# Order of the maxima's scores against the fills in four slots, and two PSUM copies, in a sliding-window attention and MLP kernel

## The chip, the cores and the metric

One Trainium2 chip, one core of it. The core has TensorE (PE; PEld are its weight loads), VectorE (DVE), ScalarE (ACT), GpSimd (POOL) and SyncE (SP), which here issues the DMAs. The metric is device time in microseconds (us) of the whole program, the median of its runs; lower is better.

## The reference

One block of a transformer: sliding-window attention over the normalized input, gated by an MLP, in float32. S is 2048 tokens, D is 512, 32 heads of 16, a window of 256, and F is 1792.

```python
xn = _layernorm(x)
# attention: 32 heads, each query sees the 256 keys up to its own
qkv = (xn @ wqkv).reshape(B, S, 3, H, Dh)          # q, k, v by heads
scores = jnp.einsum("bhqd,bhkd->bhqk", q, k) * (Dh ** -0.5)
mask = (idx[:, None] - idx[None, :] >= 0) & (idx[:, None] - idx[None, :] < W)
p = _softmax(jnp.where(mask, scores, -1e9))
s = jnp.einsum("bhqk,bhkd->bhqd", p, v).reshape(B, S, D) @ wo
# gate: a second layer norm, Dense, GELU, Dense, SiLU
h = _gelu(_layernorm(xn) @ w1 + b1)
g = _silu(h @ w2 + b2)
return x + s * g
```

## The kernel before

The program runs in two parts. The first is attention, with everything that can be done beside it; the second is the rest of the MLP, the output projection and the gate.

**Slots.** The first part is one loop over `t` from -16 to 128, and a turn of it is called a slot here. Slots 0 to 127 are eight groups of four heads (`n = t // 16`) times sixteen blocks of 128 keys (`kb = t % 16`). In the slots below 0 the input is normalized and transposed, and the first projections run. All engines get their instructions in the order in which the loop issues them (`Ordered` keeps program order), so a line's place in the loop is its place in each engine's queue.

**Scores for the exponentials.** `prob_block(n, kb, p)` makes the scores of 128 keys against up to 384 queries for two heads: two matmuls on the two halves of the PE's rows, into `stb`, one pair of PSUM banks. ACT takes the exponential into `pt`, and POOL zeroes what lies outside the window with one or two selects. There are two such blocks in a slot, `p = 1` and then `p = 0`, and both use `stb`; from slot 116 on, the block of `p = 1` uses `xy` instead.

**Maxima.** The softmax needs each query's largest score in advance, LEAD = 12 slots ahead. `max_block(n, qb)` makes scores of a block of 128 queries in four matmuls into the pair of banks `xy`. The window's far corner comes as `first_scores` into `zo`. DVE merges the corner into `xy` with a predicated copy (`COPY_PREDICATED`; in the first two blocks of a group there is no corner, and a constant is used) and reduces `xy` to the negative maximum `mt`. `own_max(t + 12)` is the call of it in slot t. The maxima's rows are split and transposed, and travel through DRAM back into the q and k buffers.

**Fills.** Between these, PE works on other products, matmul by matmul: projections of later heads' q and k, of v, and hidden rows of the MLP. They accumulate in the banks `fb[0]` and `fb[1]` (in the profile `fb`, in the program's order `fb_111` and `fb_112`). A fill is a pair of matmuls on the two halves of PE's rows, one for each bank. `fills[t, half]` holds those of a slot: half 0 stands between the two score blocks, half 1 behind the second. `by_halves` places a job's pairs in slots that are written out by hand: the q and k projection of the second group's second chunk (`job_qk(1, 1)`) has six pairs each in slot 0 (half 1), slot 1 (half 0) and slot 2 (halves 0 and 1). `tandem(t0, t1, ...)` spreads two jobs over the slots t0 to t1 and ends them in slot t1, by copying the two banks out: `fb[0]` in half 0 and `fb[1]` in half 1, both on ACT. The next pair that writes these banks waits for the copies. Spans that end in slots 19, 35 and 115 are followed by a span that starts in the next slot.

**Copies of v.** `job_v(0, 7)` ends behind the first score block, which is issued at the end of slot -1. Its two banks are copied into `vt` on ACT (the inner `finish` of `job_v`), ahead of slot 0's exponential. The first fills of slot 0 use the same banks.

**Where the maxima stand.** In a slot, PE gets the first score block, the maxima's scores, the fills of half 0, the second score block, the fills of half 1, the corner of the next maximum, and the product of the probabilities with v for the block before (`pv_step`, into `zo`). The table `MAX_BEHIND` moves the maxima's scores of a slot behind so many of its fills of half 0: 2 in slots 1, 4, 20, 36, 52, 84 and 100, and in all other slots they stand in front.

All instructions are recorded at line 43, the line of `Ordered`, so the profile's rows are told apart by their tiles. `pjr` and `hr` are the raw copies of the fills' banks (a projection, a hidden row), `sh` is the rounded high part of a projection, `oraw` the copied product with v.

Of the kernel before, what the change touches and what calls it, by code (L numbers as in the profile page):

```python
# [17 lines left out]
S, D, H, DH, WIN, F = 2048, 512, 32, 16, 256, 1792  # L18
# [5 lines left out]
NQ = H // 4  # L24
EPS = 1e-5
NEG = -3.0e38
LEAD = 12
# [23 lines left out]
def mixer_kernel(ctx, tc, x, wqk, wv, wo, w1, b1, w2, b2, out):  # L51


    nc = SimpleNamespace(**{name: Ordered(tc, name) for name in ("tensor", "vector", "scalar", "gpsimd", "sync")})
# [131 lines left out]
    fb = [psf.tile([P, 512], F32, name=f"fb{i}") for i in range(2)]  # L186
# [10 lines left out]
    vt = vp.tile([P, NKB, 16, DH + 1], F32, name="vt")  # L197
# [92 lines left out]
    fills = {}  # L290
# [95 lines left out]
    def job_v(hf, i):  # L386

        box = []

        def mm(k):  # L390
            if k == 0:
                box.append(ps_st.tile([P, 2, 256], F32, tag="b", name=f"pv_{hf}_{i}"))
            j, kt, (a, b) = k // 12, k % 12 // 3, PASSES[k % 3]
            kb = 2 * i + j
            nc.tensor.matmul(box[0][:, j], big[:, a, kt, P * kb: P * (kb + 1)], wva[:, b, kt],
                             start=(k % 12 == 0), stop=(k % 12 == 11))

        def half(bank, j, k, r, **flags):
            kt, (a, b) = k // 3, PASSES[k % 3]
            kb = 2 * i + j  # L400
            return nc.tensor.matmul(bank[:, 0:256], big[r, a, kt, P * kb: P * (kb + 1)], wva[r, b, kt], **flags)

        def finish():
            if i < 4:
                nc.scalar.copy(vt[:, 2 * i: 2 * i + 2, :, 0:DH], box[0].rearrange("p b (h d) -> p b h d", d=DH))
                return
            for j, bank in enumerate(box):
                nc.scalar.copy(vt[:, 2 * i + j, :, 0:DH], bank[:, 0:256].rearrange("p (h d) -> p h d", d=DH))
        if i > 3:
            return half, finish, box  # L410
        return [(109, mm, k) for k in range(24)], finish
# [86 lines left out]
    def tandem(t0, t1, one, two, mid=None, back=None):  # L498

        n = one[0]
        lo, hi = slice(0, 64), slice(64, P)
        mid = mid or max(1, (t0 + t1 + 1) // 2)
        most = n // 4

        def places(slots, last):

            last = min(most, n // (len(slots) + 1)) if last else 0
            cuts = [(n - last) * k // len(slots) for k in range(len(slots) + 1)]  # L510
            out = []
            for t, a, b in zip(slots, cuts, cuts[1:]):
                ahead = min(b - a, n // 3) if t < 16 * NQ - LEAD else min(b - a, max(most, (b - a + 1) // 2))
                out += [(t, 0)] * ahead + [(t, 1)] * (b - a - ahead)
            return out + [(t1, 0)] * last

        first, second = places(range(t0, mid), False), places(range(back or mid, t1), True)
        for phase, where in enumerate((first, second)):
            for i in range(n):
                flags = dict(start=(phase == 0 and i == 0), stop=(phase == 1 and i == n - 1), skip_group_check=True)  # L520
                def unit(i=i, phase=phase, flags=flags):
                    made = ((two if phase == 0 else one)[1](fb[1 - phase], i, hi, **flags),
                            (one if phase == 0 else two)[1](fb[phase], i, lo, **flags))
                    if phase == 1 and i == 0 and t0 < 16 * NQ - LEAD:
                        for r in made:
                            tc.add_manual_dep(r.ins, outs["copy"].ins.name, ORDER, reason="the banks change rows")
                fills.setdefault(where[i], []).append((unit, ()))
        fills.setdefault((t1, 0), []).append((one[2], (fb[0], t1, nc.scalar.copy)))
        if t1 >= 16 * NQ - LEAD:
            fills[t1, 0].append((two[2], (fb[1], t1, nc.vector.tensor_copy)))  # L530
            return
        ends_pair.add(t1)

        def copy(dst, src):
            outs["second"] = nc.scalar.copy(dst, src)
        fills.setdefault((t1, 1), []).append((two[2], (fb[1], t1, copy)))

    def spread(jobs, places):

# [74 lines left out]
    def prob_block(n, kb, p):  # L614
        slot = slots[n % 2]
        w = min(384, S - P * kb)
        pt = pp.tile([P, 2, 384], F32, tag="pt", name=f"pt_{n}_{kb}_{p}")
        both = xy if p and 16 * n + kb + LEAD >= 16 * NQ else stb[0]
        for a in (1, 0):
            r = slice(64 * a, 64 * a + 64)  # L620
            nc.tensor.matmul(both[:, a, 0:w], slot[r, 1, p, P * kb: P * (kb + 1)],
                             slot[r, 0, p, P * kb: P * kb + w], start=True, stop=True)
        writers[n, kb, p] = [nc.scalar.activation(pt[:, :, 0:w], both[:, :, 0:w], AF.Exp, scale=DH ** -0.5)]
        select = nc.gpsimd.affine_select(out=pt[:, :, 0:P], in_=pt[:, :, 0:P], pattern=[[0, 2], [1, P]],
                                compare_op=ALU.is_ge, fill=0.0, base=0, channel_multiplier=-1)
        if w == 384:
            select = nc.gpsimd.affine_select(out=pt[:, :, 256:384], in_=pt[:, :, 256:384],
                                             pattern=[[0, 2], [-1, P]], compare_op=ALU.is_gt, fill=0.0,
                                    base=0, channel_multiplier=1)
        writers[n, kb, p].append(select)  # L630
        pts[(n, kb, p)] = pt
# [194 lines left out]
    del fills[-11, 1][-5:]  # L826
    soon = {}
    tandem(3, 8, pair_qk(1, 2), pair_qk(1, 3))
    for n, spans in enumerate((((9, 14), (15, 19)), ((20, 24), (25, 30)), ((31, 35), (36, 41)), ((42, 47), (48, 53, 51)),
                               ((75, 79), (80, 85)), ((86, 91), (92, 97))), 2):  # L830
        for c, span in zip((0, 2), spans):
            tandem(*span[:2], pair_qk(n, c), pair_qk(n, c + 1), *span[2:])
    for i, (t0, t1) in enumerate(((54, 58), (59, 63), (64, 68), (69, 74))):
        tandem(t0, t1, pair_v(2 * i), pair_v(2 * i + 1))
# [73 lines left out]
           -10: [ln3[0][0], ln3[1][0], ln3[0][1], ln3[1][1], ln3[0][2], ln3[1][2]],  # L908
           -9: [ln3[2][0], ln3[3][0], ln3[2][1], ln3[3][1], ln3[2][2], ln3[3][2]]}

    MAX_BEHIND = {t: 2 for t in (1, 4, 20, 36, 52, 84, 100)}

    def own_max(m):
        max_block(m // 16, m % 16, m not in IN_PLACE)

    def fill_in(t, half):
        now[:] = t, half
        run(delayed.pop((t, half), ()))
        for k, (fn, args) in enumerate(fills.get((t, half), ())):
            if half == 0 and k == MAX_BEHIND.get(t):  # L920
                own_max(t + LEAD)
# [3 lines left out]
    for t in range(-16, end + 1):  # L925
# [5 lines left out]
        if 0 < t < end:  # L931
            prob_block(t // 16, t % 16, 1)
        if t >= 0 and m < end and t not in MAX_BEHIND:
            own_max(m)
# [53 lines left out]
    for f in range(6, NF, 2):  # L988
        t = gp.tile([P, 2, 512], F32, tag="ohl", name=f"hr_{f}", bufs=4)
# [451 lines left out]
```

## Time and profile before

| | us |
|---|---|
| median of 3 runs | 731.88 (731.73 to 732.29) |
| the profiled execution | 732.0 |
| its span, first to last instruction | 730.3 |

Busy time by stretch of the span, from the windows view; the granted TensorE clock is 1.00 in each:

| stretch, us | what runs | length | PE | PEld | DVE | ACT | POOL |
|---|---|---|---|---|---|---|---|
| 0 to 63.4 | slots -16 to 0 | 63.4 | 60.8 | 56.2 | 50.1 | 48.5 | 32.4 |
| 63.4 to 72.2 | slots 1 to 3 | 8.8 | 8.4 | 6.3 | 6.6 | 6.5 | 4.5 |
| 72.2 to 386.2 | slots 4 to 115 | 314.0 | 308.9 | 244.9 | 231.0 | 239.0 | 225.9 |
| 386.2 to 413.7 | slots 116 to 127 | 27.5 | 27.4 | 19.1 | 10.1 | 20.4 | 20.4 |
| 413.7 to 730.3 | the second part | 316.6 | 312.9 | 259.0 | 197.4 | 113.5 | 40.6 |

A row of the timeline gives the start in us from the span's start, the length, the engine, the operation, its tiles as out<-in with shapes, the count of merged instructions, and in brackets the idle time of that engine ahead of it with what ended it. The weight loads (PEld) show best when PE was held, since they are not modelled as matmuls' ends are. Slot 1 begins with the stb load at 63.4, slot 20 with the stb matmul at 117.0, slot 36 at 162.6, slot 115 at 383.4.

### The profile page before, as it was taken

What the parts mean: (1) busy time and instruction counts of PE and PEld (TensorE: products, weight loads), DVE (VectorE), ACT (ScalarE), POOL (GpSimd) and SP (SyncE); (2) the same over time, 40 slices, a digit from 0 to 9 for tenths busy, and PEclk for the clock granted to TensorE, in tenths of its full rate; (3) what the DMA queues carried; (4) which work ended last, traced back from release to release, by engine and by line L of the source; (5) the groups of instructions that cost most, each with busy time, mean ns of one, the idle gap of its engine ahead of it and who ended that gap; (6) DMA issues with size and microseconds to landing.
All of it is one profiled execution on the core that took longest, in us unless ns stands there. A gap on an engine that the chain in (4) does not pass through costs nothing.

```text
span 730.3 us, 19066 instructions
## 1 busy us (share of the span) xinstructions
PE 718.3 (98%) x7584; PEld 585.4 (80%) x7584; DVE 495.0 (68%) x729; ACT 427.8 (59%) x725; POOL 323.9 (44%) x683
## 2 busy tenths in 40 slices
PE   8999999999999999999999999999999999999997
PEld 7998777777778887777776788888888888888886
DVE  7886776867766777777882657446687855667823
ACT  8767777877777676878877736232343734541001
POOL 7444767767677665777876540203303000001102
PEclk9999999999999999999999999999999999999999
DMA  8324447777776733667624366347223312263801
GB/s 302 75 50 109 100 122 180 215 226 221 207 206 175 208 123 96 171 156 211 175 90 155 104 238 204 142 131 244 87 57 116 117 58 87 67 191 108 252 18 58
DMA packets 61528, 106.77 MB, mean 146 GB/s; under 512 B 12096, under 2 KB 12352, under 8 KB 61440
## 3 DMA queue, kind: packets, MB, share of 16 engines
q1 hardware_dynamic: 61440, 105.56, 49.3%
q8 instruction: 60, 0.98, 0.6%
q14 instruction: 28, 0.23, 0.1%
HBM read 54.53 MB, written 33.82 MB: 121 GB/s over the span
## 4 chain that ended last, share of the span: by engine, by line
PE 93%; ACT 3%; DVE 2%; DMA 1%; SPq 1%; issue 1%; POOL 0%; DVEq 0%; POOLq 0%
PE acc L43 21%; PE fb L43 20%; PE zo L43 14%; PE p L43 9%; PE stb L43 9%; PE s L43 6%; PE h L43 6%; PE xy L43 5%; ACT pt L43 2%; PE pv L43 2%; DVE xy L43 1%; DVE mt L43 1%; SPq L43 1%; DMA x<-in_x_dram 1%; PE tr L43 0%
## 5 line engine op out<-in xcount | busy, mean ns | idle before, releaser
L43 POOL TENSOR_SCALAR_AFFINE_SELECT pt<-pt 128x256 f32<-128x256 f32 x480 | 193.4, 428 | 96.7 <-ACT pt L43 91.1
L43 ACT ACTIVATE pt<-stb 128x768 f32<-128x768 f32 (+1 forms) x244 | 188.7, 774 | 44.0 <-PE stb L43 37.8
L43 DVE TENSOR_REDUCE mt<-xy 128x4 f32<-128x1024 f32 (+1 forms) x128 | 152.6, 1192 | 4.4
L43 DVE COPY_PREDICATED xy<-upper,zo 128x512 f32<-128x512 int32 x112 | 77.8, 695 | 73.9 <-PE xy L43 64.8
L43 POOL TENSOR_TENSOR xo<-xo,gated 128x512 f32<-128x512 f32 x15 | 20.0, 1331 | 220.4 <-DVE gated L43 219.4
L43 PE MATMUL zo<-pt,vt 128*17 128x128 f32 x2880 | 103.7, 275 | 0.0
L43 PE MATMUL fb<-xnT,wqb 64*128 64x512 f32 (+2 forms) x732 | 100.6, 382 | 0.3
L43 PE MATMUL stb<-qk 64*128 64x384 f32 (+1 forms) x488 | 94.6, 382 | 4.6 <-ACT pt L43 3.0
L43 PE MATMUL acc<-w,gh 128*128 128x512 f32 x320 | 98.5, 389 | 0.0
L43 PEld LDWEIGHTS stb<-qk 64*128 64x128 f32 x488 | 45.7, 183 | 48.1 <-ACT pt L43 39.5
L43 PEld LDWEIGHTS zo<-pt,vt 128*17 128x17 f32 x2880 | 67.5, 97 | 15.0 <-issue 5.0
L43 PEld LDWEIGHTS acc<-w,gh 128*128 128x128 f32 x320 | 60.1, 188 | 12.5
L43 PEld LDWEIGHTS fb<-xnT,wqb 64*128 64x128 f32 (+1 forms) x732 | 62.2, 185 | 7.3 <-ACT pjr L43 0.6
L43 PE MATMUL acc<-w,gl 128*128 128x512 f32 x160 | 62.2, 389 | 0.0
L43 PE MATMUL xy<-qk 64*128 64x256 f32 (+2 forms) x536 | 57.6, 288 | 0.4 <-DVE mt L43 0.2
L43 PE MATMUL p<-xnT 128*128 128x512 f32 x189 | 51.8, 389 | 0.0
L43 PEld LDWEIGHTS xy<-qk 64*128 64x128 f32 x536 | 46.8, 185 | 5.2 <-issue 2.2
L43 ACT COPY oraw<-zo 128x128 f32<-128x128 f32 x108 | 28.8, 266 | 37.5 <-PE zo L43 28.0
L43 ACT ACTIVATE gated<-acc 128x512 f32<-128x512 f32 x16 | 8.7, 596 | 61.9 <-DVE acc L43 61.9
L43 PE MATMUL s<-wos,ohl 128*128 128x512 f32 (+1 forms) x204 | 44.3, 376 | 0.0
L43 PEld LDWEIGHTS s<-wos,ohl 128*128 128x128 f32 x204 | 36.8, 188 | 7.1
L43 PEld LDWEIGHTS p<-xnT 128*128 128x128 f32 x189 | 35.5, 188 | 7.3
(206 smaller groups left out, 1193.3 us busy)
## 6 DMA issues: line engine op xcount, KB each, us to landing
qk<-sh SPq DMA_DIRECT2D x128, 128.0 KB
qk<-pjr SPq DMA_DIRECT2D x64, 128.0 KB
oT_d<-oraw SPq DMA_DIRECT2D x32, 256.0 KB
w_d<-in_w_dram SPq DMA_DIRECT2D x14, 512.0 KB
xt_d<-xnT SPq DMA_DIRECT2D x12, 512.0 KB
x<-in_x_dram SPq DMA_DIRECT2D x16, 256.0 KB
w<-w_d SPq DMA_DIRECT2D x16, 256.0 KB
or<-oT_d SPq DMA_DIRECT2D x16, 256.0 KB
```

The source lines that it names most:

```text
L43: r = issue(*args, **kwargs)
```

## The change

Three edits.

In `job_v`, the second bank of the last v job is copied by VectorE. In `tandem`, the second bank's copy is issued in half 0 when the span ends in slot 115 (spans that end later returned before this line, and LEAD is 12, so `16 * NQ - LEAD` is 116). In `MAX_BEHIND`, the maxima's scores stand behind four pairs of fills in slot 1 (two before) and in slot 2 (none before), and in front of the fills in slots 20 and 36 (behind two before). Slots 4, 52, 84 and 100 stay.

```diff
             for j, bank in enumerate(box):
-                nc.scalar.copy(vt[:, 2 * i + j, :, 0:DH], bank[:, 0:256].rearrange("p (h d) -> p h d", d=DH))
+                copy = nc.vector.tensor_copy if i == 7 and j else nc.scalar.copy
+                copy(vt[:, 2 * i + j, :, 0:DH], bank[:, 0:256].rearrange("p (h d) -> p h d", d=DH))
...
-        fills.setdefault((t1, 1), []).append((two[2], (fb[1], t1, copy)))
+        fills.setdefault((t1, int(t1 + 1 < 16 * NQ - LEAD)), []).append((two[2], (fb[1], t1, copy)))
...
-    MAX_BEHIND = {t: 2 for t in (1, 4, 20, 36, 52, 84, 100)}
+    MAX_BEHIND = {1: 4, 2: 4, 4: 2, 52: 2, 84: 2, 100: 2}
```

On DVE in slot 0, the copy stands between the reduction of the maximum of slot -1 (`mt_8`) and the predicated copy of slot 0's:

```order
 L43 COPY_PREDICATED xy<-upper,zo 128x4x128
 L43 TENSOR_REDUCE mt_8_874<-xy 128x4
+L43 COPY vt<-fb_112 128x16x16
 L43 COPY_PREDICATED xy<-upper,zo 128x4x128
 L43 TENSOR_REDUCE mt_12_1106<-xy 128x4
```

One copy is added here, and the same copy is gone from ACT, where it stood ahead of the exponential `pt_0_0` of slot 0.

On PE in slot 20, the piece between the first score block and the rest of the fills (xy are the maxima's scores, fb the fills):

```order
 L43 MATMUL stb<-qk_751 128x384 x2
-L43 MATMUL fb_112<-xnT,wqb_1900 128x512
-L43 MATMUL fb_111<-xnT,wqb_1900 128x512
-L43 MATMUL fb_112<-xnT,wqb_1900 128x512
-L43 MATMUL fb_111<-xnT,wqb_1900 128x512
 L43 MATMUL xy<-qk_94 128x128 x4
+L43 MATMUL fb_112<-xnT,wqb_1900 128x512
+L43 MATMUL fb_111<-xnT,wqb_1900 128x512
+L43 MATMUL fb_112<-xnT,wqb_1900 128x512
+L43 MATMUL fb_111<-xnT,wqb_1900 128x512
```

Two pairs of fills moved behind the four xy matmuls; slot 36 changes in the same way. In slots 1 and 2 the movement is the other way, by two pairs and by four.

On ACT in slots 115 and 116 (`hr` are the two banks' copies, `pt_3_0` the second exponential of slot 115, `pt_4_1` the first of slot 116):

```order
 L43 ACTIVATE pt_3_1_6901<-stb 128x768
 L43 COPY hr_6919<-fb_111 128x512
-L43 ACTIVATE pt_3_0_6923<-stb 128x768
-L43 COPY hr_6929<-fb_112 128x512
+L43 COPY hr_6921<-fb_112 128x512
+L43 ACTIVATE pt_3_0_6925<-stb 128x768
 L43 ACTIVATE pt_4_1_6950<-xy 128x768
```

The exponential now stands behind both copies. The other engines' orders stay as they were.

## The prediction

> **What bounds the kernel now.** I read the page's engine row first, then the waits, then the timeline of the slots that the change touches. The page's first row and its engine row, then rows of the waits view (engine, what waits, on whom: us in total, times, longest):
>
> ```profile
> span 730.3 us, 19066 instructions
> PE 718.3 (98%) x7584; PEld 585.4 (80%) x7584; DVE 495.0 (68%) x729; ACT 427.8 (59%) x725; POOL 323.9 (44%) x683
> ...
> PE stb L43 <- DMA qk<-mT_d: 0.6, 1, 0.6
> ...
> PEld stb L43 <- ACT pt L43: 39.5, 149, 0.9
> ...
> PEld xy L43 <- DVE mt L43: 1.1, 3, 0.5
> ...
> PEld fb L43 <- ACT pjr L43: 0.6, 2, 0.3
> ...
> PEld fb L43 <- ACT hr L43: 0.3, 1, 0.3
> ```
>
> PE looks busy 98% of the time, but a matmul's end is modelled, so the waits must be read at the weight loads (PEld). There the score blocks of the exponentials (stb) wait 149 times for ACT: they share one pair of banks, so block, exponential and next block alternate. The other three kinds of wait are few, and the change aims at them.
>
> How long that alternation takes is seen in slots 35 to 37, in the timeline (start, length, engine, what, idle time before it):
>
> ```profile
> 161.39 1.23 DVE L43 TENSOR_REDUCE mt<-xy 128x4 f32<-128x1024 f32 x1
> ...
> 161.77 0.82 ACT L43 ACTIVATE pt<-stb 128x768 f32<-128x768 f32 x1
> ...
> 162.64 0.44 PE L43 MATMUL stb<-qk 64*128 64x384 f32 x2 [0.18 <-ACT pt L43]
> ...
> 163.12 0.30 PEld L43 LDWEIGHTS fb<-xnT,wqb 64*128 64x128 f32 x4 [0.29 <-ACT pjr L43]
> ...
> 163.12 0.81 ACT L43 ACTIVATE pt<-stb 128x768 f32<-128x768 f32 x1
> ...
> 164.75 0.81 ACT L43 ACTIVATE pt<-stb 128x768 f32<-128x768 f32 x1 [0.31 <-PE stb L43]
> ...
> 165.62 0.18 PEld L43 LDWEIGHTS stb<-qk 64*128 64x128 f32 x2 [0.41 <-ACT pt L43]
> ```
>
> From one exponential's start to the next takes 1.35 us at least (161.77 to 163.12): 0.82 of ACT, 0.05 to release PE, 0.44 of matmuls and 0.04 back. A slot has two, so nothing goes below 2.70 us per slot. Where an exponential starts later than 1.35 us after the one before, PE or another engine was late, and only that surplus can be won. Slot 36 shows it: 164.75 - 163.12 = 1.63, a surplus of 0.28, and ACT says that it waited 0.31 for PE. PE was late because the first fill pair of the slot stood 0.29 us for ACT's copy of the bank.
>
> **Slots 0 to 2.** The rows of these slots:
>
> ```profile
> 61.76 0.65 ACT L43 COPY vt<-fb 128x256 f32<-128x256 f32 x2 [0.99 <-PE fb L43]
> ...
> 62.19 0.70 DVE L43 COPY_PREDICATED xy<-upper,zo 128x512 f32<-128x512 int32 x1 [1.20 <-PE zo L43]
> 62.41 0.81 ACT L43 ACTIVATE pt<-stb 128x768 f32<-128x768 f32 x1
> 62.46 0.77 PEld L43 LDWEIGHTS fb<-xnT,wqb 64*128 64x128 f32 x12 [0.35 <-ACT vt L43]
> ...
> 63.68 0.40 PE L43 MATMUL fb<-xnT,wqb 64*128 64x256 f32 x4
> 63.88 0.81 ACT L43 ACTIVATE pt<-stb 128x768 f32<-128x768 f32 x1 [0.66 <-PE stb L43]
> ...
> 64.20 0.30 PEld L43 LDWEIGHTS xy<-qk 64*128 64x128 f32 x4 [0.33 <-DVE mt L43]
> ...
> 65.39 0.81 ACT L43 ACTIVATE pt<-stb 128x768 f32<-128x768 f32 x1 [0.70 <-PE stb L43]
> ...
> 66.74 0.81 ACT L43 ACTIVATE pt<-stb 128x768 f32<-128x768 f32 x1
> 66.75 0.30 PEld L43 LDWEIGHTS xy<-qk 64*128 64x128 f32 x4 [0.31 <-DVE mt L43]
> ...
> 67.10 0.88 PE L43 MATMUL fb<-xnT,wqb 64*128 64x256 f32 x12
> ...
> 68.19 0.81 ACT L43 ACTIVATE pt<-stb 128x768 f32<-128x768 f32 x1 [0.65 <-PE stb L43]
> ```
>
> Here the maxima set the pace. The xy scores wait for the reduction before them in slot 1 (0.33) and slot 2 (0.31), and what is queued behind them on PE, fills and the second stb block, waits too.
>
> *Slot 0.* A VectorE copy of 256 elements from PSUM has no row. These are the nearest, from the groups by shape (count, busy, mean ns):
>
> ```profile
> L43 DVE COPY oraw<-zo 128x128 f32<-128x128 f32 x20 | 5.8, 290 | 1.9 <-PE zo L43 0.5
> ...
> L43 DVE TENSOR_TENSOR hr<-fb,scales 128x512 f32<-128x512 f32 x4 | 2.6, 686 | 16.1 <-PE fb L43 11.5 <-PE stb L43 4.6
> ```
>
> The bounds are 0.29 and 0.69; by length, 0.29 + (0.69 - 0.29) x 128/384 = 0.42, which I take. DVE is idle then and starts at 61.76, when ACT starts the first bank, so it is done at 62.18, and the predicated copy behind it moves from 62.19 by 0.02 or so (by 0.29 at the upper bound, by nothing at the lower). The fills begin at 62.22 and not at 62.46. The exponential of 62.41 keeps its place, since its block on PE comes no earlier. The next may start at 62.41 + 1.35 = 63.76, 0.12 earlier than 63.88.
>
> [...]
>
> *Slot 1.* A pair of fills costs (0.88 - 0.40)/4 = 0.12 (six pairs against two). The xy scores still wait for the reduction until about 64.2; two more pairs now run in that wait. The second block then has two pairs ahead of it and not four: 0.24 less on PE, 0.02 given back by the reduction. The exponential of 65.39 goes to 65.17, and by the alternation the one of 66.74 to 66.52.
>
> *Slot 2.* The xy scores wait until 66.77 whatever stands ahead of them. Four pairs (0.48) now run in that time, and two are left behind, so PE reaches the second block some 0.46 earlier; but the exponential can't start before 66.52 + 1.35 = 67.87. Against 68.19 that is **0.32 us**. Later slots move along: every wait in them is for work that moved too. Bounds: 0.48 if all four pairs count, about 0 if the copy takes 0.69, since both maxima then come 0.29 later.
>
> **Slots 20 and 36.** The rows of slot 20:
>
> ```profile
> 117.44 0.30 PEld L43 LDWEIGHTS fb<-xnT,wqb 64*128 64x128 f32 x4 [0.29 <-ACT pjr L43]
> ...
> 117.44 0.81 ACT L43 ACTIVATE pt<-stb 128x768 f32<-128x768 f32 x1
> ...
> 117.84 0.36 PEld L43 LDWEIGHTS xy<-qk 64*128 64x128 f32 x4
> ...
> 119.08 0.81 ACT L43 ACTIVATE pt<-stb 128x768 f32<-128x768 f32 x1 [0.31 <-PE stb L43]
> ...
> 120.70 0.81 ACT L43 ACTIVATE pt<-stb 128x768 f32<-128x768 f32 x1
> ```
>
> Both slots follow a slot in which ACT has just copied two banks of fills, and the new fills wait 0.29 for the second copy. The four xy scores need none of that. Put first, they run while the fills wait, and the wait disappears. They need the reduction of the maximum before, which in slot 36 ends at 161.39 + 1.23 = 162.62, before PE has started the block ahead of them at 162.64; so I cost the added wait at nothing. The second exponential is then bound by the alternation: 117.44 + 1.35 = 118.79 against 119.08, **0.29**; 163.12 + 1.35 = 164.47 against 164.75, **0.28**. [...]
>
> **Slot 115.** Its rows, and the first of slot 116:
>
> ```profile
> 384.85 0.59 ACT L43 COPY hr<-fb 128x512 f32<-128x512 f32 x1
> ...
> 385.33 0.82 ACT L43 ACTIVATE pt<-stb 128x768 f32<-128x768 f32 x1
> ...
> 386.03 0.59 ACT L43 COPY hr<-fb 128x512 f32<-128x512 f32 x1
> ...
> 386.23 0.19 PEld L43 LDWEIGHTS xy<-qk 64*128 64x128 f32 x2 [0.49 <-DVE mt L43]
> ...
> 386.68 0.52 PEld L43 LDWEIGHTS fb<-xnT 64*128 64x128 f32 x6 [0.27 <-ACT hr L43]
> ...
> 387.24 0.19 PEld L43 LDWEIGHTS stb<-qk 64*128 64x128 f32 x2
> ```
>
> The second copy moves from 386.03 to 385.33 and ends at 385.92. The fills of slot 116 then don't wait: **0.27**. The exponential moves back by 0.48 (385.33 - 384.85, what a copy holds ACT) to 385.81 and ends at 386.63. What needs it is the next stb block, loaded at 387.24 - 0.27 = 386.97: 0.34 to spare, so the delay costs nothing. The block on xy at 386.23 waits for DVE as before. Without that margin the delay would cost up to 0.14; the bounds are 0.1 and 0.3. From here to the end PE sets the time.
>
> **The sum.** 0.32 + 0.29 + 0.28 + 0.27 = 1.16 us off the span: 730.3 becomes 729.1. The profiled execution took 732.0 and the median is 731.88, so the same difference gives 730.72, say **730.7**. All low ends together give 731.8, all high ends (0.48 + 0.35 + 0.35 + 0.3 = 1.48) 730.4.
>
> **Rivals.**
>
> *More is won.* The exponential of 120.70 comes 1.62 after the one before, a surplus of 0.27. If that was a late effect of the same stall, it goes as well; with the high ends in slots 0 to 2 and 115 the sum is 0.48 + 0.29 + 0.27 + 0.28 + 0.3 = 1.62, so 730.3. For it: a PE that is ahead finds its operands ready. Against it: that exponential follows a full block of probability-times-v matmuls, which do not shrink.
>
> *Swallowed later.* PE waits once for a DMA (0.6, the maxima's rows on their way back into the buffer). If SP's queue ahead of it keeps its own time, the first three terms end there and only slot 115's stays: 731.6. Against it: the transfers in that queue are sent by ACT, POOL and PE work that moved too.
>
> *The swap does nothing.* If PE could run the xy scores past the waiting fills already, slots 20 and 36 win nothing: 0.32 + 0.27, so 731.3. The xy loads start at 117.84, behind the fills that waited until 117.44, which speaks against it. [...]
>
> *Slower.* The xy scores in front of slots 20 and 36 take away the slack that a late maximum had. If DVE arrives there one maximum late (0.70 + 1.23 = 1.93), PE stands 1.8 us in place of 0.29, with the fills and the second stb block behind it: 1.5 lost in each slot, 3.0 together, less the 0.32 and 0.27 of the other places, so +2.4 and 734.3. It decides from a reduction that ends some 0.7 us later than now in both slots. For it: PE waited for reductions three times, 1.1 us. Against it: in both slots the reduction has just ended.
>
> **How the numbers follow.** Forecast 0.52, more 0.30, swallowed 0.03, nothing from the swap 0.03, slower 0.12. The forecast's own range is 730.3 to 731.2. A change under 0.2% (1.46 us) is about what a measurement here can't tell from none; that line lies at 730.42, so a quarter of the forecast (0.13) and all of "more" are faster: 0.43. Same: 0.39 + 0.06 = 0.45. Slower: 0.12. The range, 729.9 to 732.0, takes in the cases up to the swallowed one and the execution's own spread; "slower" is left out.
>
> **What would show it.** Right: no wait of fb for pjr in slots 20 and 36 and for hr in 116; no wait of fb for vt beyond some 0.1 us in slot 0; the vt copy on DVE at about 0.42; exponentials 1.35 apart in slots 1, 2, 20 and 36; slot 3 some 0.3 us earlier, slot 37 some 0.9, slot 117 some 1.2. Wrong: a new wait of xy for mt in slots 20 or 36, a wait of stb 116 for the exponential of 115, or gains that shrink between slot 37 and slot 115.

## The result, and the profile after

The changed kernel takes 730.89 us (median of 22 runs, 730.48 to 733.14), the one before 731.91 beside it: 1.02 less, a ratio of 0.9987 with a 95% interval from 0.9981 to 0.9993. That is less than 0.2%; the time lies in the range of the prediction, 0.2 us above its forecast. The profiled execution took 731.04 us with a span of 729.3; before, 732.0 and 730.3.

The head of the page of the changed kernel, then rows of its waits (engine, what waits, on whom: us in total, times, longest):

```profile
span 729.3 us, 19068 instructions
PE 718.0 (98%) x7584; PEld 586.6 (80%) x7584; DVE 496.2 (68%) x730; ACT 427.6 (59%) x724; POOL 324.1 (44%) x683
```

```profile
PEld stb L43 <- ACT pt L43: 39.6, 150, 0.8
...
PEld zo L43 <- DVE xy L43: 3.8, 15, 0.6
...
PEld xy L43 <- DVE mt L43: 0.7, 2, 0.5
```

One instruction went from ACT to DVE. The waits of fb for pjr and for hr are gone, and xy waits for the reduction twice and not three times. The alternation of stb and the exponentials is as it was.

The sum can be checked place by place, since a trace holds the start of every exponential. The table gives how much earlier than before an exponential starts, differenced over each place, so that what happened ahead of the place drops out:

| place | forecast | changed kernel | the same, executed again |
|---|---|---|---|
| slots 0 to 2 | 0.32 | 0.15 | 0.14 |
| slot 20 | 0.29 | 0.07 | 0.07 |
| slot 36 | 0.28 | 0.17 | 0.09 |
| slots 115, 116 | 0.27 | 0.27 | 0.28 |
| slots 60, 61 | 0 | 0.28 | 0.29 |
| from slot 0 to slot 117, all | 1.16 | 0.99 | 0.96 |

The total is right, its parts are not: three terms gave between a quarter and three fifths of what was forecast, and 0.28 came from a place that the change doesn't touch. (In slot 98 a score block waits for a transfer, 0.63 us in the execution before and 0.58 in the changed one; this slot makes the rest.)

**Slots 0 to 2.** Timeline of the changed kernel (start, length, engine, what, idle time before it):

```profile
61.79 0.38 ACT L43 COPY vt<-fb 128x256 f32<-128x256 f32 x1 [0.99 <-PE fb L43]
...
61.89 0.42 DVE L43 COPY vt<-fb 128x256 f32<-128x256 f32 x1 [0.88 <-PE fb L43]
...
62.37 0.78 PEld L43 LDWEIGHTS fb<-xnT,wqb 64*128 64x128 f32 x12 [0.23 <-DVE vt L43]
...
63.80 0.81 ACT L43 ACTIVATE pt<-stb 128x768 f32<-128x768 f32 x1 [0.55 <-PE stb L43]
...
64.78 0.70 DVE L43 COPY_PREDICATED xy<-upper,zo 128x512 f32<-128x512 int32 x1 [0.48 <-PE xy L43]
...
65.19 0.81 ACT L43 ACTIVATE pt<-stb 128x768 f32<-128x768 f32 x1 [0.58 <-PE stb L43]
...
65.52 0.30 PEld L43 LDWEIGHTS zo<-qk 64*128 64x128 f32 x4 [0.64 <-DVE xy L43]
...
66.72 0.81 ACT L43 ACTIVATE pt<-stb 128x768 f32<-128x768 f32 x1
...
68.07 0.81 ACT L43 ACTIVATE pt<-stb 128x768 f32<-128x768 f32 x1 [0.54 <-PE stb L43]
```

And two rows of the kernel before that the prediction did not show:

```profile
64.74 0.69 DVE L43 COPY_PREDICATED xy<-upper,zo 128x512 f32<-128x512 int32 x1 [0.48 <-PE xy L43]
...
65.49 0.30 PEld L43 LDWEIGHTS zo<-qk 64*128 64x128 f32 x4 [0.41 <-DVE xy L43]
```

The exponential of 65.39 comes at 65.19, where 65.17 was forecast. But then PE reaches the corner scores (zo), which wait for the predicated copy of slot 1. That copy ends at 64.78 + 0.70 = 65.48, no earlier than before (64.74 + 0.69 = 65.43); so PE waits 0.64 and not 0.41, starts the corner at 65.52 (before 65.49), and the next exponential stands at 66.72 (before 66.74). The gain of slot 1 became a longer wait. Only slot 2 keeps something: 66.72 + 1.35 = 68.07.

**Slots 20 and 36.** Slot 20, then slot 36, in the timeline of the changed kernel:

```profile
116.79 0.19 PEld L43 LDWEIGHTS stb<-qk 64*128 64x128 f32 x2 [0.46 <-ACT pt L43]
...
117.19 0.33 PEld L43 LDWEIGHTS xy<-qk 64*128 64x128 f32 x4 [0.21 <-DVE oraw L43]
...
117.28 0.81 ACT L43 ACTIVATE pt<-stb 128x768 f32<-128x768 f32 x1
117.41 0.79 PEld L43 LDWEIGHTS fb<-xnT,wqb 64*128 64x128 f32 x8
...
118.84 0.81 ACT L43 ACTIVATE pt<-stb 128x768 f32<-128x768 f32 x1 [0.25 <-PE stb L43]
...
162.46 0.19 PEld L43 LDWEIGHTS stb<-qk 64*128 64x128 f32 x2 [0.46 <-ACT pt L43]
...
162.75 0.33 PEld L43 LDWEIGHTS xy<-qk 64*128 64x128 f32 x4
...
162.94 0.81 ACT L43 ACTIVATE pt<-stb 128x768 f32<-128x768 f32 x1
162.97 0.80 PEld L43 LDWEIGHTS fb<-xnT,wqb 64*128 64x128 f32 x8
...
164.41 0.81 ACT L43 ACTIVATE pt<-stb 128x768 f32<-128x768 f32 x1
```

The fills no longer wait, but xy is late itself: it starts 0.40 and 0.29 after the stb block ahead of it, where most slots have 0.11. The exponentials stand 1.56 and 1.47 apart, not 1.35. What PE does in between is seen in its records in the trace, where the wait instructions of its sequencer stand too (start, length):

```
116.790 0.051 EVENT_SEMAPHORE
116.791 0.183 LDWEIGHTS stb<-qk
116.901 0.051 EVENT_SEMAPHORE
117.007 0.051 EVENT_SEMAPHORE
117.113 0.051 EVENT_SEMAPHORE
117.189 0.182 LDWEIGHTS xy<-qk
```

Four wait instructions stand ahead of xy in the program, 0.106 to 0.111 us from one to the next (three in slot 36). They wait for transfers into the buffer that the scores read, all of which had landed by then, as experiment five shows. Before, the same four ran from 117.45 on, while the first fill pairs were on PE.

**Slots 115 and 116.** The same view:

```profile
384.15 1.07 ACT L43 COPY hr<-fb 128x512 f32<-128x512 f32 x2
...
385.12 0.83 ACT L43 ACTIVATE pt<-stb 128x768 f32<-128x768 f32 x1
...
385.53 0.19 PEld L43 LDWEIGHTS xy<-qk 64*128 64x128 f32 x2 [0.50 <-DVE mt L43]
...
385.64 0.60 PEld L43 LDWEIGHTS fb<-xnT 64*128 64x128 f32 x6
...
386.28 0.19 PEld L43 LDWEIGHTS stb<-qk 64*128 64x128 f32 x2
```

Both copies run in one piece, the fills of 385.64 and the stb block of 386.28 wait for nobody: as forecast.

**Slots 60 and 61.** The kernel before, then the changed one:

```profile
233.87 0.27 ACT L43 COPY oraw<-zo 128x128 f32<-128x128 f32 x1 [0.96 <-PE stb L43]
...
234.19 1.02 PEld L43 LDWEIGHTS fb<-wva,xnT 64*128 64x128 f32 x16 [0.30 <-ACT oraw L43]
```

```profile
233.22 0.27 ACT L43 COPY oraw<-zo 128x128 f32<-128x128 f32 x1 [0.68 <-PE zo L43]
...
233.54 1.01 PEld L43 LDWEIGHTS fb<-wva,xnT 64*128 64x128 f32 x16
```

Before, ACT's copy of oraw comes 0.28 later than its like, and the fills wait 0.30 for it. The wait instruction ahead of the copy ends at 233.56 before and at 233.18 after; the copy starts 0.32 and 0.04 behind it. All that it waits for was done by then, in both kernels. So ACT itself was late, and this went away with the change.

### The profile page after: what moved, and what is told of

It reads as the page before. It is cut to its first block, busy times and chain, and to the rows that moved or that the text cites. A ratio compares the mean times of both kernels' runs of the same rounds, so it can differ in the third digit from the quotient of the medians.

```text
span 729.3 us, 19068 instructions
## 1 busy us (share of the span) xinstructions
PE 718.0 (98%) x7584; PEld 586.6 (80%) x7584; DVE 496.2 (68%) x730; ACT 427.6 (59%) x724; POOL 324.1 (44%) x683
## 4 chain that ended last, share of the span: by engine, by line
PE 93%; ACT 3%; DVE 1%; DMA 1%; SPq 1%; issue 1%; POOL 0%; DVEq 0%; POOLq 0%
PE acc L43 21%; PE fb L43 20%; PE zo L43 14%; PE p L43 9%; PE stb L43 9%; PE s L43 6%; PE h L43 6%; PE xy L43 5%; ACT pt L43 2%; PE pv L43 2%; DVE xy L43 1%; SPq L43 1%; DMA x<-in_x_dram 1%; DVE mt L43 0%; PE tr L43 0%
```

## The experiments

Eleven experiments ran, in three series; each is compared with the kernel before in its own series (731.93 for one to four, 731.92 for five to eight, 731.85 for nine to eleven). Single parts are worth less than an interval is wide (some 0.7 us to each side), so the starts of the exponentials decide. "Slots 0 to 2" and so on in the results are differenced as in the table above.

**One: the vt copy alone.**

```diff
-                nc.scalar.copy(vt[:, 2 * i + j, ...], ...)
+                copy = nc.vector.tensor_copy if i == 7 and j else nc.scalar.copy
+                copy(vt[:, 2 * i + j, ...], ...)
```

> The kernel before with one part of the change: the copy of the second vt bank in slot 0 is done by VectorE; the score order and the copy of slot 115 are as before. Theory A (ScalarE's instruction stream): before, ScalarE's copy of slot 60 starts 0.32 us after its last wait ends, where its like starts 0.04 after; that delay belongs to the place of the instruction in ScalarE's stream, and with one ScalarE instruction fewer it falls on the exponential of slot 61, which waits for PE anyway. Then slots 0 to 60 gain at most 0.1 us, slot 61 steps by 0.3, and the whole kernel gains 0.3. Rival B (chance of one execution): no step in slot 61, or steps of this size in other slots, and the kernel gains less than 0.1. The recorded step: VectorE's copy takes 0.42, the fills begin 0.24 earlier and the exponential of 63.88 comes 0.12 earlier.

731.58 us, ratio 0.9994 (0.9985 to 1.0003). The exponential of 63.88 comes 0.11 earlier against the start of slot 0, as forecast, but this is lost by the next one: slots 0 to 2 give -0.01. Slots 60 and 61 give 0.29; slot 12 takes 0.14, which no other run shows (there the corner scores waited 0.15 for the predicated copy). So what this part is worth in the trace lies 170 us behind it.

**Two: the scores of slots 1 and 2 alone.**

```diff
-    MAX_BEHIND = {t: 2 for t in (1, 4, 20, 36, 52, 84, 100)}
+    MAX_BEHIND = {1: 4, 2: 4, 4: 2, 20: 2, 36: 2, 52: 2, 84: 2, 100: 2}
```

> The kernel before with four pairs of fills ahead of the maximum's scores in slots 1 and 2, nothing else. The recorded prediction: the second exponential of slot 1 comes 0.2 us earlier, the one after it too, and slots 3 and on 0.3 earlier. Theory A (corner scores): in slot 1 PE's gain is handed to the four corner scores, which wait for the predicated copy of the maximum, and that copy doesn't move; the first exponential of slot 2 stays within 0.05 of its place, the second comes 0.12 earlier by the alternation, and all later slots keep 0.10 to 0.15. The delay of ScalarE's copy in slot 60 stays as it was, so no step in slot 61. Total: -0.3 by the prediction, -0.1 by theory A.

731.80 us, ratio 1.0001 (0.9992 to 1.0009). Slots 0 to 2 give 0.16, slots 60 and 61 nothing. Its timeline:

```profile
65.17 0.81 ACT L43 ACTIVATE pt<-stb 128x768 f32<-128x768 f32 x1 [0.54 <-PE stb L43]
65.42 0.30 PEld L43 LDWEIGHTS zo<-qk 64*128 64x128 f32 x4 [0.56 <-DVE xy L43]
...
66.62 0.81 ACT L43 ACTIVATE pt<-stb 128x768 f32<-128x768 f32 x1
...
67.97 0.81 ACT L43 ACTIVATE pt<-stb 128x768 f32<-128x768 f32 x1 [0.54 <-PE stb L43]
```

65.17 is 0.22 earlier than before, 66.62 only 0.12: the corner took the rest. The term of slots 0 to 2 is this one part.

**Three: slots 20 and 36 alone.**

```diff
-    MAX_BEHIND = {t: 2 for t in (1, 4, 20, 36, 52, 84, 100)}
+    MAX_BEHIND = {t: 2 for t in (1, 4, 52, 84, 100)}
```

> The kernel before with the maximum's scores of slots 20 and 36 in front of the fills, nothing else. The recorded prediction: 0.29 and 0.28 us, together 0.57. Theory A (wait instructions): the scores carry four and three wait instructions for long finished transfers; PE's sequencer needs 0.106 us for each, which before ran while the first fill pairs kept PE busy; in front they stand bare, the scores start 0.40 and 0.29 after the stb block and not 0.11 after, and the gains are 0.1 in slot 20 and 0.15 to 0.2 in slot 36, together 0.25 to 0.3. No step in slot 61, since ScalarE's instructions are as before.

731.61 us, ratio 0.9993 (0.9984 to 1.0002). Slot 20 gives 0.07, slot 36 0.18, slots 60 and 61 nothing; xy starts 0.40 and 0.29 after the stb block. (Slots 0 to 2, not touched here, show -0.10 in this execution: so much a single execution can be off there.)

**Four: slot 115 alone.**

```diff
-        fills.setdefault((t1, 1), []).append((two[2], (fb[1], t1, copy)))
+        fills.setdefault((t1, int(t1 + 1 < 16 * NQ - LEAD)), []).append((two[2], (fb[1], t1, copy)))
```

> The kernel before with the copy of the second hr bank in slot 115 ahead of the second exponential, nothing else. The recorded prediction: nothing moves until slot 115, its second exponential comes 0.5 us later, the fills of slot 116 don't wait for the copy, the second exponential of slot 116 comes 0.27 earlier, and the total is 0.27 less. Rival (the delayed exponential is waited for): the stb block of slot 116 waits for ScalarE and 0.13 or less is left. The ScalarE delay in slot 60 stays.

731.59 us, ratio 0.9994 (0.9985 to 1.0003). Slots 115 and 116 give 0.27, with the second exponential of 115 later by 0.45 against the one ahead of it, and none of the other places gives more than 0.02 but slot 98.

**Five: the wait instructions taken over elsewhere.** The changed kernel and

```diff
+        if t in (19, 35):
+            slot = slots[(t + 13) // 16 % 2]
+            nc.tensor.matmul(zo[0:1, 1, 400:402], slot[0:64, 0, 0, 0:1], slot[0:64, 1, 0, 0:2], start=True, stop=True)
         if t >= 0 and m + 1 < end and (m + 1) % 16 >= 2 and m + 1 not in IN_PLACE:
             first_scores((m + 1) // 16, (m + 1) % 16)
```

> The changed kernel and, in slots 19 and 35 ahead of the corner scores, one matmul of one row by two columns into unused PSUM columns that reads the same buffers as the maximum's scores of the next slot, so that it takes over their wait instructions (four and three). Theory A (wait instructions cost 0.106 us each when they stand bare): in slots 20 and 36 the scores start 0.11 us after the stb block and not 0.40 and 0.29 after; the second exponentials come 1.35 after the first ones; slot 21 gains 0.2 and slot 37 another 0.1, so 0.3 in all against the changed kernel, 1.3 against the one before. Rival B (the scores wait for something real at that moment, a transfer or VectorE's copy of oraw): the scores stay 0.40 and 0.29 behind the stb block and nothing is gained. Rival C: the wait instructions cost as much where they are now, and the gain is 0 or below.

730.67 us, ratio 0.9983 (0.9974 to 0.9992). Its timeline in slots 19 and 20:

```profile
115.71 0.08 PEld L43 LDWEIGHTS zo<-qk 64*1 64x1 f32 x1 [0.21 <-DVE xy L43]
...
116.72 0.18 PEld L43 LDWEIGHTS stb<-qk 64*128 64x128 f32 x2 [0.32 <-ACT pt L43]
...
116.75 0.29 DVE L43 COPY oraw<-zo 128x128 f32<-128x128 f32 x1
116.83 0.36 PEld L43 LDWEIGHTS xy<-qk 64*128 64x128 f32 x4
...
117.20 1.19 PE L43 MATMUL fb<-xnT,wqb 64*128 64x512 f32 x8
117.21 0.81 ACT L43 ACTIVATE pt<-stb 128x768 f32<-128x768 f32 x1
...
118.61 0.81 ACT L43 ACTIVATE pt<-stb 128x768 f32<-128x768 f32 x1
```

xy follows the stb block by 0.11 in both slots, which are now worth 0.23 each. So the wait instructions had cost 0.16 and 0.06 (0.14 in slot 36 by the second execution of the changed kernel); together 0.22 is won where 0.3 was expected. Nothing real was waited for. The small matmul passes the same four waits between 115.31 and 115.71, over 1 us before xy, and they follow each other by 0.106 there too, so the transfers had landed. VectorE's copy of oraw, which the view of the changed kernel names, isn't needed either: here it runs from 116.75 to 117.05, and xy starts at 116.83. The second exponential comes 1.40 after the first (1.41 in slot 36): what is left above 1.35 is PE's own work, 1.19 of fills behind xy.

**Six and seven: one more ScalarE instruction,** in the kernel before and in the changed one:

```diff
     at(62, nc.sync.dma_start, b1s, b1)
+    behind(26, nc.scalar.copy, sv[:, 29:30], mhalf[:, 0:1])
```

> The kernel before with one more ScalarE instruction: a copy of one column (into a column of sv that nothing reads then) at the end of slot 26, where ScalarE idles. Nothing of the change is in it. Theory A (ScalarE's instruction stream): every instruction behind it moves by one place, the 0.28 us delay of slot 60 falls on the wait instruction ahead of the copy, which waits 1.4 us anyway, and slot 61 and all later ones come 0.3 earlier: the kernel is 0.3 us faster though it has more to do. Rival B (chance, or a cause on another engine): slot 61 as before, total the same or up to 0.1 slower.

> The changed kernel with the same one-column ScalarE copy at the end of slot 26. Theory A: the copy of slot 60 has its old place in ScalarE's stream again, starts 0.3 us after its last wait ends, and slots 61 and on come 0.3 later than in the changed kernel; against the kernel before the gain is 0.7 and not 1.0. Rival B: no step in slot 61, the gain stays 1.0.

The kernel before with it: 731.63 us, ratio 0.9997 (0.9988 to 1.0005); slots 60 and 61 give 0.29, of the other places only slot 98 anything. The changed kernel with it: 731.09 us, ratio 0.9987 (0.9978 to 0.9996); slots 60 and 61 give 0.00, the other places what they gave without it. The median of seven against the changed kernel can't tell 0.3; the copy of slot 60 can. Its row in six, with a second row from slot 36, and then in seven:

```profile
165.42 0.27 ACT L43 COPY oraw<-zo 128x128 f32<-128x128 f32 x1 [0.32 <-DVE mT L43]
...
233.10 0.27 ACT L43 COPY oraw<-zo 128x128 f32<-128x128 f32 x1 [0.68 <-PE zo L43]
```

```profile
233.54 0.27 ACT L43 COPY oraw<-zo 128x128 f32<-128x128 f32 x1 [0.96 <-PE stb L43]
...
233.85 1.02 PEld L43 LDWEIGHTS fb<-wva,xnT 64*128 64x128 f32 x16 [0.30 <-ACT oraw L43]
```

Counting ScalarE's records in the trace in order of time, wait instructions among them, the place decides in all thirteen executions:

| the copy of slot 60 is ScalarE's record number | kernels | it starts behind its wait |
|---|---|---|
| 447 | the changed one (both executions), one, five, eight | 0.04 |
| 448 | before, two, three, four, seven | 0.32 |
| 449 | six, nine, ten | 0.04 |

In six the late row of 165.42 is ScalarE's record 320, 128 places ahead of 448; it starts 0.32 behind its wait too, and so in nine and ten, and costs nothing, for the exponential behind it waits for PE in any case.

**Eight: the corner scores behind the probability-times-v matmuls of slot 1.** The changed kernel and

```diff
-        if t >= 0 and m + 1 < end and (m + 1) % 16 >= 2 and m + 1 not in IN_PLACE:
+        corner = t >= 0 and m + 1 < end and (m + 1) % 16 >= 2 and m + 1 not in IN_PLACE
+        if corner and t != 1:
             first_scores((m + 1) // 16, (m + 1) % 16)
         if t >= 1:
             pv_step((t - 1) // 16, (t - 1) % 16)
+        if corner and t == 1:
+            first_scores((m + 1) // 16, (m + 1) % 16)
```

> The changed kernel with the four corner scores of slot 1 behind the probability-times-v matmuls of that slot and not ahead of them. Theory A (the corner scores' wait for the predicated copy swallowed slot 1's gain): the matmuls no longer stand behind the wait of 0.64 us, the stb block of slot 2 comes earlier and its first exponential starts 1.35 after the one before, so 0.15 to 0.2 earlier; slots 2 to 19 keep 0.15 to 0.2, and against the changed kernel 0.15 is gained in all. Rival B (the maxima's own chain on VectorE sets slots 2 and 3): slot 2's first exponential comes earlier, but slot 3 and later ones stay, nothing gained.

Neither came. 731.32 us, ratio 0.9990 (0.9982 to 0.9999), and slots 0 to 2 give -0.25, 0.40 less than in the changed kernel. Its timeline:

```profile
64.80 0.70 DVE L43 COPY_PREDICATED xy<-upper,zo 128x512 f32<-128x512 int32 x1 [0.48 <-PE xy L43]
...
65.61 0.16 PEld L43 LDWEIGHTS zo<-pt,vt 128*17 128x17 f32 x8 [0.71 <-POOL sv L43]
...
66.11 0.27 ACT L43 COPY oraw<-zo 128x128 f32<-128x128 f32 x1
...
66.42 0.30 PEld L43 LDWEIGHTS zo<-qk 64*128 64x128 f32 x4 [0.66 <-ACT oraw L43]
```

Whichever goes first waits for the predicated copy: the program has a wait for it ahead of the matmuls too, since they write the tile zo that the copy reads, though other columns of it. (The view names POOL's memset, which ended at the same time, 65.50.) Then the corner waits again, for the copy of oraw out of the same tile. So the wait can't be moved by order alone; that the copy's end sets PE's next step stands, since PE was held to it in both orders. That slot 1 would keep its gain without this wait is not shown: no run takes the wait away.

**Nine and ten: no vt copy on VectorE.** The changed kernel with the vt copy on ScalarE again and the one-column copy of six; ten has the small matmuls of five as well.

> The changed kernel with the copy of the second vt bank on ScalarE again, as before, and the one-column ScalarE copy at the end of slot 26. Theory A (moving the vt copy pays only by taking one instruction out of ScalarE's stream): the added copy shifts the stream as well, slot 61 still steps by 0.3 against the kernel before, and slots 0 to 2 give their 0.15 without VectorE's copy; the gain is that of the changed kernel, 1.0 within 0.2. Rival B (the earlier fills of slot 0 are needed for the gain of slots 1 and 2): slots 0 to 2 give nothing, the gain is 0.85 or less.

> The same, with the small matmuls in slots 19 and 35 that take over the wait instructions. Theory A: 0.2 to 0.3 less than the kernel without them, 1.2 to 1.3 less than before, and about as fast as the changed kernel with the small matmuls.

Nine: 731.05 us, ratio 0.9987 (0.9978 to 0.9996): slots 0 to 2 give 0.06, slots 60 and 61 0.29. Ten: 730.68 us, ratio 0.9984 (0.9975 to 0.9993): slots 0 to 2 give 0.17, slots 20 and 36 0.23 and 0.22, slots 60 and 61 0.29. Of the two values for slots 0 to 2, nine's is low by a 0.10 that is lost ahead of slot 1; its gain by the medians, 0.80, fits rival B as well as theory A, so nine alone doesn't decide. Ten's 0.17, and the 0.16 of experiment two, show that VectorE's copy isn't needed for that term. Five and ten are the fastest kernels here, 1.25 and 1.17 us below the one before; against the changed kernel's 1.02 that is no difference by the medians, and 0.2 by the places.

**Eleven: the changed kernel again.**

> The changed kernel unaltered, a second profiled execution beside the first: what repeats is the program's, what doesn't is chance. By theory A the scores of slots 20 and 36 start 0.40 and 0.29 after the stb block again, ScalarE's copy of slot 60 starts 0.04 after its wait, and the gain is 1.0. The stb block of slot 98, which waits 0.58 for a transfer in the first execution, is expected to differ by 0.2 or so from execution to execution.

730.99 us, ratio 0.9990 (0.9982 to 0.9999). The table above has its places. xy of slot 20 is 0.40 behind the stb block again, that of slot 36 0.38, not 0.29, which is why this slot gave 0.09: two of its wait instructions stand 0.20 apart and not 0.106, for a reason that the trace doesn't show. In slot 98 it gives 0.13, as all other kernels do; only the execution of before and the first one after waited there for a transfer.

One thing the differences leave out: the first exponential of slot 0 starts between 59.5 and 60.8 us in these executions. The changed kernel alone shows 59.99 and 60.82. That spread lies ahead of everything in this case, and is in every median.

## Why the prediction was right, and where it was wrong

The forecast of 730.7 met 730.89, with four terms of which one had the right size, and a fifth cause that it did not have.

- *The vt copy* took the 0.42 that was worked out. But VectorE began 0.10 after ScalarE and not beside it, so the fills started at 62.37 and not 62.22, after a wait of 0.23, where the prediction allowed some 0.1. It made no difference: the gain of 0.11 in the next exponential was gone one exponential later (experiment one).
- *Slots 1 and 2, 0.32 forecast, 0.15 measured.* The step that failed reads "and by the alternation the one of 66.74 to 66.52". The exponential ahead of it did come at 65.19. But the alternation is a lower bound, and PE had to pass the corner scores first, whose wait for the predicated copy (0.41 in the trace of before) was left out. It grew to 0.64. The step for slot 2, four pairs in the wait and then 1.35, held.
- *Slots 20 and 36, 0.57 forecast, 0.24 measured (0.16 in the second execution).* The wait of the fills went away, as forecast, and the reduction was in time; but the exponentials stand 1.56 and 1.47 apart, not 1.35. The step that failed is "so I cost the added wait at nothing". There was no added wait for data, but four and three wait instructions whose issue had been hidden by the fills. With these taken away the slots are worth 0.46; the last 0.11, some 0.05 in each slot, is lost because eight fills behind xy make PE, not the alternation, the bound, 1.40 in place of 1.35. No run shows the 0.35 that the sum of the high ends counts for each of the two slots: the runs gave between 0.07 and 0.23 in each.
- *Slot 115, 0.27 forecast, 0.27 measured,* with its margin: the delayed exponential wasn't waited for.
- *Not foreseen: 0.28 in slots 60 and 61.* An instruction taken off ScalarE's stream in slot 0 took a delay of 0.28 us off a copy that the fills wait for. The exponential behind the copy then has its number, 448; it starts at 233.53, 0.04 behind the copy's end, and shows no delay.

Some 0.5 too much in three terms, and 0.28 in slots 60 and 61 and 0.06 in slot 98 left out: the errors cancel down to 0.17, 0.99 in place of 1.16. The total was met in part by luck.

Of the rivals: "more is won" wanted the surplus of 120.70 to go; in the changed kernel that exponential stands 1.62 behind the one before it, as before. "Swallowed later" wanted the gains to shrink; they stay constant within 0.04 from slot 3 to 19, 37 to 59 and 62 to 97. "The swap does nothing" falls with experiment three, which wins 0.25 by the swap alone: in the kernel before, PE had not run the scores past the waiting fills. "Slower" wanted xy to wait for a late reduction in slots 20 and 36; no such wait appeared.

## What to carry to other kernels

Before an instruction is costed at nothing in its new place, count the wait instructions that it carries along: behind queued fills they cost nothing here, and bare they held the scores up by 0.29 and 0.18, of which 0.16 and 0.06 reached the next exponential. "By the alternation" is only a bound; walk through each wait between one exponential and the next, and look which of them ends at a time that doesn't move. A gain or loss of a few tenths in a place that the edit doesn't touch can come from the mere number of instructions ahead of it on an engine, as the 0.28 in slots 60 and 61 did here; before explaining it, add or take one idle instruction and see whether it goes.

## What the runs showed of the hardware

A wait instruction on PE's sequencer has a record of 0.051 us (all 164 in the kernel before). Ahead of xy in slots 20 and 36 of the changed kernel the next one follows 0.106 to 0.111 after it; a step of 0.20 stands in slot 36 of the kernel before (163.24 to 163.44) and of the second execution of the changed one. Four in a row in slot 20 put xy 0.40 behind the stb block, 0.29 more than the 0.11 of most slots.

ScalarE's records 320 (in six, nine and ten) and 448 (in the kernel before, two, three, four and seven) started 0.32 us behind a wait that had ended, 0.28 later than others, and the delay went with the number: the copies that hold records 319, 322, 447 or 449 in other kernels don't have it. A third such place, 384 behind the second, shows in nine and ten: a cast into gh, in the second part, is record 832 there and starts 0.32 behind its wait; the same cast is record 830 in the kernel before and 831 in four, and starts 0.04 behind. So the three late places stand 128 and 384 apart. The delay cost nothing at record 320, where the exponential behind the copy waited for PE, and 0.28 us in slot 60, where the fills waited for the late copy. What the delay is, no run shows. In the execution before, 28 packets of 8 KB start within the span on queue q14, of the kind "instruction", and the trace doesn't tell for which engine. Four of them start at 168.28, 234.71, 305.18 and 368.44 us, when ScalarE had begun 322, 449, 575 and 704 records, some 128 apart; but these four were picked out of the 28, and whether they have to do with the delay was not tested.
